# Half 1's keys parked in scratch, and the feed-forward start, splits and late norms put in another order

## The chip, the cores and the metric

The kernel runs on one core of a Trainium2 chip. TensorE (PE) multiplies matrices into PSUM, VectorE (DVE), ScalarE (ACT) and GpSimd (POOL) work on tiles, and SyncE (SP) issues the DMAs, in program order. The metric is the device time of one launch in microseconds (us). Three runs of the kernel before took 3108.89, 3109.24 and 3113.45 us.

## The reference

A transformer block whose norms are scaled and shifted by rows from a condition `c`: attention of 32 query heads over 16 key/value heads (the last 512 cached positions of 2048), then a gated feed-forward network. x is 2048 x 576, Dh is 128, F is 4608, all float32.

```python
q = (x @ wq) ... ; k, v = last W = 512 positions of the caches, each for two query heads
o = softmax(q k^T * Dh ** -0.5) v ; attention = o @ wo
h = sigmoid(x @ w_gate) * (x @ w_up) ; ffn = h @ w_down
...
mod = silu(c) @ w_mod                    # sa, ca, ga, sb, cb, gb
x = x + ga * attention(layernorm(x) * (1 + ca) + sa)
x = x + gb * ffn(layernorm(x) * (1 + cb) + sb)
```

## The kernel before

The 2048 rows are four blocks of 512. Every float32 matmul is made of three products of a "hi" part (the value rounded to fp32r) and a "lo" part (the rest): hi times hi, hi times lo, lo times hi. So each operand is split: mostly ACT copies it to hi and DVE or POOL subtracts to get lo.

**Attention** runs in two halves, half 0 for blocks 0 and 1, half 1 for blocks 2 and 3. A half goes through 32 heads, and the work of one head and one block (a "block step") is four steps n; `at_n(n, fn)` (L426 to L501) lists what is issued besides at step n: loads of weights, splits, norms. A group gg is one key/value head of one half. `load_k` and `load_v` fetch it from the caches, `make_k` (`prep_k`) transposes the keys on PE (L330) and splits them into the tile `kt`, `make_v` splits the values into `vs`. Both halves do this for all 16 heads. At the same time background jobs read the feed-forward weights, form their sums, split them and store them in scratch (`wsc` for gate and up, `dsc` for down).

**Feed-forward** runs in two pairs of blocks, pair 0 and pair 1, with a Strassen-like scheme: seven combinations of the norm's quadrants ("combos" 0 to 6, in the order B11, B21, T1, T2, B22, T3, T4) and seven combinations of the weights. Scratch `scr[pair][c]` holds combo c in rows. `stage` (L741) loads it in two halves into tiles `ts` (three buffers), and `load_combo` (L749) transposes it on PE (L756, twelve transposes), copies to hi on ACT (L757) and subtracts to lo on DVE (L759), giving the tile `hc`. A unit u (36 for each pair) makes seven products (`product`, seven matmuls of 512 columns at L882) from weight tiles `sw` and the `hc` of one combo, into PSUM tiles a, b and c; after two of the seven matmuls it also issues a down-projection (`down`, three matmuls of 288 columns, operands `sd` and `hl`, added on DVE at L854). `keep` copies a PSUM tile to SBUF on ACT (L889); L1003 and L1016 are the sigmoids.

Two units give the four value quadrants A11, A12, A21, A22. `sum_val` forms S1 to S4 from them on POOL (L818), and `split_val` splits values and sums into `hl`: hi on ACT (L812), lo on POOL (L813).

**Pair 1's norm.** `late_stats` (L893) makes the mean and the reciprocal root of blocks 2 and 3 at the end of unit 0, in two chains of 128x4 operations on DVE (L166 to L182), and stores the blocks (`park_x`, L566). `late_tile` (L901) normalises one of four tiles ahead of units 4, 9, 14 and 19 and stores its combos into `scr[1]`.

A scheduler may move instructions on an engine, except those that `pin` or `keep_order` hold in written order. Here the ACT instructions of the feed-forward part are free.

Of the kernel before, what the change touches and what calls it, by code (L numbers as in the profile page):

```python
# [16 lines left out]
P = 128  # L17
# [7 lines left out]
def adaln_block_kernel(ctx: ExitStack, tc: tile.TileContext, x, k_cache, v_cache, wq, wo, w_gate, w_up, w_down,  # L25
# [529 lines left out]
    PH = {}  # L555

# [131 lines left out]

    def mod_make2(key, m, j, add):
        if j == 0:  # L690
            rows2[key] = mod_rows(key + "2", wp if key == "gate" else const)
        mod_make(rows2[key], m, j, add)
# [48 lines left out]
    def stage(pair, c):  # L741
        halves = []
        for i in range(2):
            t = fh.tile([P, 2, D3], F32, tag="ts", name="ts", bufs=3)
            nc.sync.dma_start(t, scr[pair][c][:, 2 * i : 2 * i + 2, :])
            halves.append(t)
        STG[pair, c] = halves

    def load_combo(pair, c):  # L749
        halves = STG.pop((pair, c))  # L750
        hc = fh.tile([P, 5, BLK], F32R, tag="hc", name="hc", bufs=7)
        HC[c] = hc
        for s in range(3):
            p = fpsum("w", 4, [P, BLK])
            for i in range(TPB):
                nc.tensor.transpose(p[:, i * P : (i + 1) * P], halves[i // 2][:, i % 2, s * P : (s + 1) * P], ident)  # L756
# [52 lines left out]
    def split_val(g, a):  # L809
        v = VAL[g, a]  # L810
        hl = fp.tile([P, 2, BLK], F32R, tag="hl", name="hl", bufs=7)
        nc.scalar.activation(hl[:, 0, :], v, AF.Copy)  # L812
        nc.gpsimd.tensor_sub(hl[:, 1, :], v, f32(hl[:, 0, :]))  # L813
        HL[g, a] = hl
# [58 lines left out]
    def product(u, a, c, p, first, downs=(2, 5)):  # L873
        w, h = SW.pop((u, a)), HC[c]
        pairs = []
        for s in range(2):
            pairs.append((w[:, 2 * s, :], h[:, 3 + s, :]))
            pairs.append((w[:, 2 * s + 1, :], h[:, s, :]))
            pairs.append((w[:, 2 * s, :], h[:, s, :]))
        pairs.append((w[:, 4, :], h[:, 2, :]))  # L880
        for n, (l, r) in enumerate(pairs):
            nc.tensor.matmul(p, l, r, start=first and n == 0, stop=n == len(pairs) - 1, skip_group_check=not first)  # L882
            if n in downs:
                down_some(1)
        load_w()

    def keep(p, tag, bufs):
        t = val(tag, bufs)
        nc.scalar.activation(t, p, AF.Copy)  # L889
        return t  # L890


    def late_stats():  # L893
        for b in range(HB, NB):
            for t in range(TPB):
                ln_stats(b, t, True)
            ln_rsqrt(b)
            park_x(b)

    def late_tile(t):  # L900
# [5 lines left out]
        for i, h in enumerate((h0, h1)):  # L906
            mv, y = LN[HB + i]
            nc.vector.tensor_scalar(h, h, mv[:, t, 0:1], y[:, t : t + 1], op0=OP.subtract, op1=OP.mult)
            nc.gpsimd.tensor_mul(h, h, rows2["scale"])
            nc.gpsimd.tensor_add(h, h, rows2["shift"])  # L910
# [7 lines left out]
        put(0, h0[:, lo])  # L918
        put(1, h0[:, hi])
        nc.gpsimd.tensor_sub(ts_[:, lo], h1[:, lo], h0[:, lo])  # L920
        nc.gpsimd.tensor_sub(ts_[:, hi], h1[:, hi], ts_[:, lo])
        put(2, ts_[:, lo])
        put(3, ts_[:, hi])
        put(4, h1[:, hi])
        nc.gpsimd.tensor_sub(h1[:, lo], h1[:, hi], h1[:, lo])
        put(5, h1[:, lo])
        nc.gpsimd.tensor_sub(h0[:, lo], h0[:, hi], ts_[:, hi])
        put(6, h0[:, lo])

    stage(0, 0)  # L930
    stage(0, 1)
    for c in range(7):
        load_combo(0, c)
        if c + 2 < 7:
            stage(0, c + 2)
        if c:
            load_w()
    for _ in range(4):
        load_w()
# [3 lines left out]
    back = later = None  # L943
    for u in range(U + 1):
        pair = u // NF
        nxt = (u + 1) // NF if (u + 1) % NF == 0 and u + 1 < U else None
        if u in (4, 9, 14, 19):
            late_tile((u - 4) // 5)
# [6 lines left out]
        def swap(c, to):  # L955
            if to:
# [11 lines left out]
        if u > 0:  # L968
# [10 lines left out]
            elif u % 2:  # L979
# [23 lines left out]
        nc.scalar.activation(g0, g0, AF.Sigmoid)  # L1003
# [12 lines left out]
        nc.scalar.activation(g1, g1, AF.Sigmoid)  # L1016
# [4 lines left out]
        if u == 0:  # L1021
            late_stats()
# [8 lines left out]
        else:  # L1031
# [3 lines left out]
            split_val(g, S1)  # L1035
# [30 lines left out]
```

## Time and profile before

| what | number |
|---|---|
| median of three runs | 3109.24 us |
| the profiled execution | 3113.13 us |
| its span | 3111.3 us |
| opening, attention half 0, half 1 | 0 to 60, to about 830, to 1833 us |
| feed-forward pairs 0 and 1 | 1833 to 2460, to 3111 us |
| waits ended by ACT for tile c at L882, all units | 11.4 us |
| HBM read, written | 357.83 MB, 140.48 MB |

The span is what the engines' instructions cover; the execution's own time is 1.8 us longer. In the profile a row of the timeline gives the start, the length, the engine, the line, the operation with its tiles and the count; what stands in brackets is the engine's idle time before the row and what ended it. Where PE has no such bracket for a long stretch, the time of that stretch is PE's work.

### The profile page before, as it was taken

What the parts mean: (1) busy time and instruction counts of PE and PEld (TensorE: products, weight loads), DVE (VectorE), ACT (ScalarE), POOL (GpSimd) and SP (SyncE); (2) the same over time, 40 slices, a digit from 0 to 9 for tenths busy, and PEclk for the clock granted to TensorE, in tenths of its full rate; (3) what the DMA queues carried; (4) which work ended last, traced back from release to release, by engine and by line L of the source; (5) the groups of instructions that cost most, each with busy time, mean ns of one, the idle gap of its engine ahead of it and who ended that gap; (6) DMA issues with size and microseconds to landing.
All of it is one profiled execution on the core that took longest, in us unless ns stands there. A gap on an engine that the chain in (4) does not pass through costs nothing.

```text
span 3111.3 us, 49123 instructions
## 1 busy us (share of the span) xinstructions
PE 3058.9 (98%) x17012; PEld 2646.9 (85%) x17012; DVE 2161.7 (69%) x4202; ACT 1432.4 (46%) x2862; POOL 1517.0 (49%) x1610
## 2 busy tenths in 40 slices
PE   7999999999999999999999999999999999999998
PEld 6888888888888888888888877888888888888887
DVE  7777777777888777777777776555555665555556
ACT  4656655555555555555555542232332323323332
POOL 3656655555333545565565505653443444434444
PEclk9999999999999999999999999999999999999999
DMA  4566655665312345444444446886666776666663
GB/s 130 160 168 159 168 156 155 161 160 155 106 31 72 96 116 152 126 119 118 114 124 116 114 166 200 279 254 198 197 199 198 220 247 198 199 198 199 201 198 119
DMA packets 564728, 501.58 MB, mean 161 GB/s; under 512 B 181504, under 2 KB 444672, under 8 KB 563456
## 3 DMA queue, kind: packets, MB, share of 16 engines
q1 hardware_dynamic: 564480, 498.44, 55.5%
q8 instruction: 135, 2.21, 0.3%
q14 instruction: 113, 0.93, 0.1%
HBM read 357.83 MB, written 140.48 MB: 160 GB/s over the span
## 4 chain that ended last, share of the span: by engine, by line
PE 90%; issue 3%; DMA 2%; DVE 2%; POOL 2%; ACT 1%; SPq 0%; POOLq 0%; DVEq 0%; ACTq 0%
PE a L882 14%; PE qp L256 13%; PE wo L256 12%; PE w L256 12%; PE ot L256 11%; PE st L256 11%; PE c L882 7%; PE st L387 7%; PE b L882 3%; POOL hl L813 0%; DVE xp L854 0%; PE st L330 0%; DMA sw<-wsc 0%; POOL vs L818 0%; DMA xp<-in_A_x_dram 0%
## 5 line engine op out<-in xcount | busy, mean ns | idle before, releaser
L854 DVE TENSOR_TENSOR xp<-w,xp 128x288 f32<-128x288 f32 x980 | 443.9, 456 | 464.4 <-PE w L256 463.2
L256 PE MATMUL wo<-wb,ov 128*128 128x288 f32 x3072 | 616.3, 308 | 2.2 <-DVE ov L405 1.2
L390 ACT ACTIVATE ptt<-st 128x512 fp32r<-128x512 f32 x512 | 305.8, 597 | 634.0 <-PE st L387 633.6
L256 PEld LDWEIGHTS w<-sd,hl 128*128 128x128 f32 x3036 | 513.8, 189 | 89.5 <-POOL hl L813 4.9
L882 PE MATMUL a<-hc,sw 128*128 128x512 f32 x2016 | 583.6, 394 | 3.1 <-DVE v L1019 2.2
L256 PE MATMUL w<-sd,hl 128*128 128x288 f32 x3036 | 565.4, 296 | 3.3 <-POOL hl L813 2.8
L414 DVE SCALAR_TENSOR_TENSOR xp<-wo,rs,xp 128x288 f32<-128x288 f32 x1024 | 513.6, 512 | 56.8 <-PE wo L256 8.8
L369 DVE TENSOR_REDUCE neg<-st 128x1 f32<-128x512 f32 x512 | 351.9, 687 | 276.5 <-PE st L256 275.4
L256 PEld LDWEIGHTS wo<-wb,ov 128*128 128x128 f32 x3072 | 482.3, 189 | 51.2 <-DVE ov L405 1.9
L256 PE MATMUL qp<-hTm,wa 128*128 128x512 f32 x1536 | 445.1, 398 | 4.2 <-ACT wa L219 1.4
L256 PE MATMUL ot<-ptt,vs 128*128 128x512 f32 x1536 | 443.8, 396 | 0.1
L256 PE MATMUL st<-kt,qt 128*128 128x512 f32 x1536 | 437.5, 393 | 0.2 <-DVE ptt L391 0.2
L882 PEld LDWEIGHTS a<-hc,sw 128*128 128x128 f32 x2016 | 355.9, 188 | 42.5 <-DVE v L1019 3.4
L375 ACT ACTIVATE pp<-st,neg 128x512 f32<-128x512 f32 x512 | 350.5, 685 | 55.6 <-DVE neg L369 54.6
L662 POOL TENSOR_TENSOR xp<-xp 128x896 fp32r<-128x896 f32 (+2 forms) x135 | 260.6, 1931 | 201.7 <-ACT xp L657 189.8
L391 DVE TENSOR_TENSOR ptt<-st,ptt 128x512 fp32r<-128x512 f32 x512 | 348.3, 680 | 5.3 <-ACT ptt L390 5.2
L256 PEld LDWEIGHTS st<-kt,qt 128*128 128x128 f32 x1536 | 287.5, 188 | 63.0 <-DVE ptt L391 1.0
L882 PE MATMUL c<-hc,sw 128*128 128x512 f32 x1008 | 306.1, 397 | 11.4 <-ACT v L889 11.4
L387 PEld LDWEIGHTS st<-ident,pp 128*128 128x128 f32 x2048 | 254.0, 139 | 73.0 <-ACT pp L375 5.9
L387 PE MATMUL st<-ident,pp 128*128 128x128 f32 x2048 | 306.5, 272 | 2.8 <-ACT pp L375 2.8
L256 PEld LDWEIGHTS qp<-hTm,wa 128*128 128x128 f32 x1536 | 262.0, 189 | 30.9 <-DVE qt L353 2.1
L256 PEld LDWEIGHTS ot<-ptt,vs 128*128 128x128 f32 x1536 | 259.6, 188 | 23.2 <-DVE ptt L391 0.3
(135 smaller groups left out, 3585.9 us busy)
## 6 DMA issues: line engine op xcount, KB each, us to landing
sw<-wsc SPq DMA_DIRECT2D x504, 320.0 KB
sd<-dsc SPq DMA_DIRECT2D x249, 288.0 KB
wsc<-xp SPq DMA_DIRECT2D x144, 448.0 KB
dsc<-xp SPq DMA_DIRECT2D x102, 336.0 KB
raw<-in_A_wo_dram SPq DMA_DIRECT2D x64, 288.0 KB
raw<-in_A_wq_dram SPq DMA_DIRECT2D x64, 256.0 KB
wsc<-xp SPq DMA_DIRECT2D x144, 112.0 KB
ts<-scr SPq DMA_DIRECT2D x28, 384.0 KB
```

What stands on the lines that cost most here:

```text
L256: nc.tensor.matmul(p, l, r, start=first and n == 0, stop=last and n == len(pairs) - 1)
L369: nc.vector.tensor_reduce(NEG[b][:, i : i + 1], p, axis=AX.X, op=OP.max, negate=True)
L375: keep_order(nc.scalar.activation(PP[n], ST.pop(n), AF.Exp, bias=NEG[b][:, i : i + 1], accum_out=SUM[b][:, i : i + 1]))
L387: nc.tensor.transpose(p[:, k * P : (k + 1) * P], PP[n][:, k * P : (k + 1) * P], ident)
L390: keep_order(nc.scalar.activation(PT[b][:, 0, :, cols], pv_, AF.Copy))
L391: nc.vector.tensor_sub(PT[b][:, 1, :, cols], pv_, f32(PT[b][:, 0, :, cols]))
L414: nc.vector.scalar_tensor_tensor(xv, p, RS[b][:, i : i + 1], xv, op0=OP.mult, op1=OP.add)
L662: pin(nc.gpsimd.tensor_sub(v[:, :n].bitcast(F32R), v[:, :n], hi[:, :n]))
L854: nc.vector.tensor_add(acc, p, acc)
L882: nc.tensor.matmul(p, l, r, start=first and n == 0, stop=n == len(pairs) - 1, skip_group_check=not first)
```

## The change

Five parts, which touch each other in the order of the code.

1. Half 0 stores each split key and value tile to scratch (`park_k`, `park_v`), and half 1 fetches them (`fetch_k` eleven steps ahead, `fetch_v` eight) in place of loading, transposing and splitting again.
2. Combos 0 to 2 of pair 0 are loaded at steps N-8 to N-6 into the space of `xp[0]` (`stage_early`). At the start of the feed-forward part `park_x` of blocks 2 and 3 stands ahead of the loads, only combos 0 and 1 are transposed up front, and in unit 0 each product is followed by the transposes of the combo two further on. The first seven `sd` loads go out ahead of the `ts` of combos 5 and 6.
3. All ACT instructions of the feed-forward part are pinned.
4. The splits of S1 to S4 are collected in `later` and issued behind v1's keep. In the last group of a pair the down-projections go by value for the first three.
5. `late_stats` and `late_tile` are one generator, `late_work`; `late_some` issues one of its operations behind each product (two in unit 1), and the root chain runs once, eight wide. In pair 1's staging a fourth buffer (`rows_ss`, which held the scale and shift rows) takes every fourth half.

```diff
@@ -448,17 +448,34 @@
+    kscr = dram.tile([HKV, P, 2, W], F32, tag="kscr", name="kscr")
+    vscr = dram.tile([HKV, P, 2, KT, DH], F32, tag="vscr", name="vscr")
+
     def load_k(gg):
-        KR[gg] = load_kv(k_cache, gg % HKV)
+        KR[gg] = load_kv(k_cache, gg)
 
     def make_k(gg):
         KS[gg] = prep_k(KR.pop(gg))
 
+    def park_k(gg):
+        keep_order(nc.sync.dma_start(kscr[gg], f32(KS[gg])))
+
+    def fetch_k(gg):
+        KS[gg] = at.tile([P, 2, W], F32R, tag="kt", name="kt", bufs=2)
+        keep_order(nc.sync.dma_start(f32(KS[gg]), kscr[gg - HKV]))
...
+    def park_v(gg):
+        keep_order(nc.sync.dma_start(vscr[gg], f32(VS[gg])))
+
+    def fetch_v(gg):
+        VS[gg] = at.tile([P, 2, KT, DH], F32R, tag="vs", name="vs", bufs=2)
+        keep_order(nc.sync.dma_start(f32(VS[gg]), vscr[gg - HKV]))
...
     for gg in range(2 * HKV):
         n = TPB * first_g[gg]
+        if gg >= HKV:
+            at_n(n - 11, fetch_k, gg)
+            at_n(n - 8, fetch_v, gg)
+            continue
+        at_n(n + 2, park_k, gg)
+        at_n(n + 3, park_v, gg)
...
+    first_ts = {}
+
+    def stage_early(c):
+        v = xp[0].rearrange("p b t d -> p (b t d)")[:, c * TPB * D3 : (c + 1) * TPB * D3]
+        v = v.rearrange("p (t d) -> p t d", t=TPB)
+        pin(nc.sync.dma_start(v, scr[0][c]))
+        first_ts[c] = [v[:, 0:2], v[:, 2:4]]
+
+    for c_ in range(3):
+        at_n(N - 8 + c_, stage_early, c_)
...
+            if pair and (2 * c + i) % 4 == 3:
+                t = rows_ss.rearrange("p a d -> p (a d)")[:, : 2 * D3].rearrange("p (t d) -> p t d", t=2)
+            else:
+                t = fh.tile([P, 2, D3], F32, tag="ts", name="ts", bufs=3)
...
-            nc.scalar.activation(hc[:, s, :], p, AF.Copy)
+            pin(nc.scalar.activation(hc[:, s, :], p, AF.Copy))
...
+        late_some(2 if u == 1 else 1)
         load_w()
...
     def late_stats():
-        for b in range(HB, NB):
+        for i in range(HB):
             for t in range(TPB):
-                ln_stats(b, t, True)
-            ln_rsqrt(b)
-            park_x(b)
+                st = const.tile([P, 2, 6], F32, tag="st", name="st", bufs=2)
+                for j in range(2):
+                    yield nc.vector.bn_stats(st[:, j, :], xs[HB + i][:, t, j * D2 : (j + 1) * D2])
+                nc.vector.bn_aggr(mv_l[:, i * TPB + t, :], st)
+            LN[HB + i] = mv_l[:, i * TPB : (i + 1) * TPB], y_l[:, i * TPB : (i + 1) * TPB]
+        v = fp.tile([P, 2 * TPB], F32, name="v_l")
+        a = fp.tile([P, 2 * TPB], F32, name="a_l")
+        yield nc.vector.tensor_scalar(v, mv_l[:, :, 1], EPS, None, op0=OP.add)
+        yi, vi = y_l.bitcast(I32), v.bitcast(I32)
+        yield nc.vector.tensor_scalar(yi, vi, 1, None, op0=OP.logical_shift_right)
+        yield nc.vector.tensor_scalar(yi, yi, -1.0, float(0x5F3759DF), op0=OP.mult, op1=OP.add)
+        for _ in range(3):
+            yield nc.vector.tensor_mul(a, y_l, y_l)
+            yield nc.vector.scalar_tensor_tensor(a, a, -0.5, v, op0=OP.mult, op1=OP.mult)
+            yield nc.vector.scalar_tensor_tensor(y_l, a, 1.5, y_l, op0=OP.add, op1=OP.mult)
...
+    def late_some(k):
+        for _ in range(k):
+            i = next(late, None)
+            if i is not None:
+                pin(i)
...
+    for c_ in first_ts:
+        STG[0, c_] = first_ts[c_]
+    for b in range(HB, NB):
+        park_x(b)
+    stage(0, 3)
+    for c_ in range(2):
+        load_combo(0, c_)
+    for _ in range(5):
+        load_w()
+    stage(0, 4)
+    for _ in range(5):
         load_w()
     for _ in range(7):
         load_sd()
...
+    def split_later():
+        for ga in later:
+            split_val(*ga)
+        later.clear()
...
-        if u in (4, 9, 14, 19):
-            late_tile((u - 4) // 5)
...
+            if u == 0 and c + 2 < 7:
+                load_combo(0, c + 2)
+                if 5 <= c + 4 < 7:
+                    stage(0, c + 4)
...
                 sum_val(g, S3, "-", A11, A21)
-                split_val(g, S3)
+                later.append((g, S3))
             else:
                 VAL[g, A12] = v
                 split_val(g, A12)
-                split_val(g, S2)
                 sum_val(g, S4, "-", A12, S2)
-                if g % NG == NG - 1 or g == GL - 1:
-                    split_val(g, S4)
+                later += [(g, S1), (g, S2), (g, S4)]
+                if g == GL - 1:
+                    split_later()
                     todo += [(g, a, t) for t in range(TPB) for a in ORDER]
+                elif g % NG == NG - 1:
+                    todo += [(g, a, t) for a in ORDER[:3] for t in range(TPB)]
+                    todo += [(g, a, t) for t in range(TPB) for a in ORDER[3:]]
                 else:
-                    later = g
                     todo += [(g, a, t) for a in ORDER for t in range(TPB)]
...
         v1 = keep(pc, "v1", 2)
-        if later is not None:
-            split_val(later, S4)
-            later = None
+        split_later()
...
-        if u == 0:
-            late_stats()
...
             sum_val(g, S1, "+", A21, A22)
-            split_val(g, S1)
             sum_val(g, S2, "-", S1, A11)
```

On PE, where attention ends and feed-forward begins. `wo` is the out-projection, L756 the transposes of combo rows, L882 the products. Before:

```order
L256 MATMUL wo<-wb,ov 128x288 x27
L756 MATMUL w<-ident,ts 128x128 x16
L882 MATMUL a<-hc,sw 128x512
L756 MATMUL w<-ident,ts 128x128 x2
L882 MATMUL a<-hc,sw 128x512 x4
L756 MATMUL w<-ident,ts 128x128 x6
L882 MATMUL a<-hc,sw 128x512 x2
L756 MATMUL w<-ident,ts 128x128 x12
L882 MATMUL b<-hc,sw 128x512 x6
```

The same place in the changed kernel, where these lines are L794 and L920, and `xp_109` holds the early combos:

```order
L256 MATMUL wo<-wb,ov 128x288 x27
L794 MATMUL w<-ident,xp_109 128x128 x36
L794 MATMUL w<-ident,ts 128x128 x4
L920 MATMUL a<-hc,sw 128x512 x7
L920 MATMUL b<-hc,sw 128x512 x7
L794 MATMUL w<-ident,ts 128x128 x4
L920 MATMUL c<-hc,sw 128x512
L794 MATMUL w<-ident,ts 128x128 x4
L920 MATMUL c<-hc,sw 128x512 x6
L794 MATMUL w<-ident,ts 128x128 x6
```

The transposes of three combos now stand in one piece ahead of all products, and two whole products follow without any between them.

On SP at the same place, the queue of DMAs. Before, from the third half tile on:

```order
L745 DMA ts<-scr_260 128x768
L779 DMA sw<-wsc_266 128x640
L745 DMA ts<-scr_260 128x768 x3
L779 DMA sw<-wsc_266 128x640
L745 DMA ts<-scr_260 128x768
L779 DMA sw<-wsc_266 128x640 x2
L745 DMA ts<-scr_260 128x768 x3
L779 DMA sw<-wsc_266 128x640 x4
L802 DMA sd<-dsc_275 128x576 x7
```

In the changed kernel, where L590 is `park_x`:

```order
L590 DMA xscr_266<-xp_110 128x2304
L783 DMA ts<-scr_262 128x768
L590 DMA xscr_267<-xp_110 128x2304
L783 DMA ts<-scr_262 128x768
L817 DMA sw<-wsc_269 128x640 x5
L783 DMA ts<-scr_262 128x768
L817 DMA sw<-wsc_269 128x640 x2
L783 DMA ts<-scr_262 128x768
L817 DMA sw<-wsc_269 128x640 x3
L840 DMA sd<-dsc_278 128x576 x7
L817 DMA sw<-wsc_269 128x640 x2
L783 DMA ts<-scr_262 128x768 x2
```

Both stores of blocks 2 and 3 (1152 KB each) moved ahead of the first weight tile, and the seven `sd` loads moved ahead of the last two half tiles shown, which are combo 5's.

On ACT, behind the border of the pairs, the last splits of pair 0. Before:

```order
L889 ACTIVATE g_28290<-a 128x512
L812 ACTIVATE hl<-g_28089 128x512
L812 ACTIVATE hl<-vs 128x512 x2
L1003 ACTIVATE g_28290<-g_28290 128x512
L889 ACTIVATE v_28381<-c 128x512
L889 ACTIVATE g_28405<-a 128x512
```

In the changed kernel, with L850 for L812, L928 for L889 and L1084 for L1003:

```order
L928 ACTIVATE g_28116<-a 128x512
L850 ACTIVATE hl<-g_27912 128x512
L1084 ACTIVATE g_28116<-g_28116 128x512
L928 ACTIVATE v_28204<-c 128x512
L850 ACTIVATE hl<-vs 128x512 x3
L928 ACTIVATE g_28234<-a 128x512
```

The splits of the sums (`vs`) moved from ahead of the sigmoid and v1's keep to behind both.

More of the change, by code (lines that the diff above doesn't have):

```diff
@@ L555, in adaln_block_kernel @@
     PH = {}
+    rows_ss = const.tile([P, 2, D], F32, name="rows_ss")
     def early_norm(t):
@@ L687, in adaln_block_kernel @@
         at_n(n + 8, bg_store, k, 1)
+    first_ts = {}
[6 more added lines that the diff above has]
+        at_n(N - 8 + c_, stage_early, c_)
     def mod_make2(key, m, j, add):
         if j == 0:
-            rows2[key] = mod_rows(key + "2", wp if key == "gate" else const)
+            rows2[key] = mod_rows("gate2", wp) if key == "gate" else rows_ss[:, 0 if key == "scale" else 1, :]
         mod_make(rows2[key], m, j, add)
@@ L811, in split_val @@
         hl = fp.tile([P, 2, BLK], F32R, tag="hl", name="hl", bufs=7)
-        nc.scalar.activation(hl[:, 0, :], v, AF.Copy)
+        pin(nc.scalar.activation(hl[:, 0, :], v, AF.Copy))
         nc.gpsimd.tensor_sub(hl[:, 1, :], v, f32(hl[:, 0, :]))
@@ L888, in keep @@
         t = val(tag, bufs)
-        nc.scalar.activation(t, p, AF.Copy)
+        pin(nc.scalar.activation(t, p, AF.Copy))
         return t
+    mv_l = const.tile([P, 2 * TPB, 2], F32, name="mv_l")
+    y_l = const.tile([P, 2 * TPB], F32, name="y_l")
     def late_stats():
-        for b in range(HB, NB):
+        for i in range(HB):
             for t in range(TPB):
-                ln_stats(b, t, True)
-            ln_rsqrt(b)
-            park_x(b)
+                st = const.tile([P, 2, 6], F32, tag="st", name="st", bufs=2)
[18 more added lines that the diff above has]
+                pin(i)
     def late_tile(t):
@@ L908, in late_tile @@
             nc.vector.tensor_scalar(h, h, mv[:, t, 0:1], y[:, t : t + 1], op0=OP.subtract, op1=OP.mult)
-            nc.gpsimd.tensor_mul(h, h, rows2["scale"])
-            nc.gpsimd.tensor_add(h, h, rows2["shift"])
+            yield nc.gpsimd.tensor_mul(h, h, rows2["scale"])
+            yield nc.gpsimd.tensor_add(h, h, rows2["shift"])
         def put(c, v):
@@ L918, in late_tile, with late_work @@
         put(0, h0[:, lo])
+        yield nc.gpsimd.tensor_sub(ts_[:, lo], h1[:, lo], h0[:, lo])
         put(1, h0[:, hi])
-        nc.gpsimd.tensor_sub(ts_[:, lo], h1[:, lo], h0[:, lo])
-        nc.gpsimd.tensor_sub(ts_[:, hi], h1[:, hi], ts_[:, lo])
         put(2, ts_[:, lo])
+        yield nc.gpsimd.tensor_sub(ts_[:, hi], h1[:, hi], ts_[:, lo])
         put(3, ts_[:, hi])
         put(4, h1[:, hi])
-        nc.gpsimd.tensor_sub(h1[:, lo], h1[:, hi], h1[:, lo])
+        yield nc.gpsimd.tensor_sub(h1[:, lo], h1[:, hi], h1[:, lo])
         put(5, h1[:, lo])
-        nc.gpsimd.tensor_sub(h0[:, lo], h0[:, hi], ts_[:, hi])
+        yield nc.gpsimd.tensor_sub(h0[:, lo], h0[:, hi], ts_[:, hi])
         put(6, h0[:, lo])
[L930 to L938, printed above, removed]
+        for _ in range(3):
+            yield None
+    def late_work():
+        yield from late_stats()
+        for t in range(TPB):
+            yield from late_tile(t)
+    late = late_work()
+    for c_ in first_ts:
[9 more added lines that the diff above has]
+    for _ in range(5):
         load_w()
@@ L941, in adaln_block_kernel @@
         load_sd()
-    back = later = None
+    back, later = None, []
+    def split_later():
+        for ga in later:
+            split_val(*ga)
+        later.clear()
     for u in range(U + 1):
@@ L1002, in adaln_block_kernel @@
         nc.vector.tensor_add(g0, pb, g0)
-        nc.scalar.activation(g0, g0, AF.Sigmoid)
+        pin(nc.scalar.activation(g0, g0, AF.Sigmoid))
         product(u, S1, T1, pc, True, downs)
@@ L1015, in adaln_block_kernel @@
         nc.vector.tensor_add(g1, pc, g1)
-        nc.scalar.activation(g1, g1, AF.Sigmoid)
+        pin(nc.scalar.activation(g1, g1, AF.Sigmoid))
         product(u, S3, T3, pa, False, downs)
```

3 lines of the change are left out of this document (1 added, 2 removed).

## The prediction

> **What bounds the kernel now.** I read the page's shares first, then the chain of waits, then the stretches, and last PE's timeline where a stretch isn't full. The two lines below are the busy time of each engine and the engines' shares of the chain that ended last.
>
> ```profile
> PE 3058.9 (98%) x17012; PEld 2646.9 (85%) x17012; DVE 2161.7 (69%) x4202; ACT 1432.4 (46%) x2862; POOL 1517.0 (49%) x1610
> PE 90%; issue 3%; DMA 2%; DVE 2%; POOL 2%; ACT 1%; SPq 0%; POOLq 0%; DVEq 0%; ACTq 0%
> ```
>
> PE is busy in all but 52.4 of 3111.3 us, so time falls only with matmul work that goes, or with one of these idle stretches and the low clock behind it. The next rows are stretches: from:to, length, then busy time (and count) of PE, PE's loads, DVE, ACT and POOL, granted clock, DMA share, GB/s.
>
> ```profile
> 140.00:300.00 160.00, 158.82 (x906) 137.19 (x906) 120.25 (x224) 97.24 (x203) 91.83 (x107) 1.00 0.64 167
> 940.00:1760.00 820.00, 819.99 (x4685) 710.11 (x4684) 628.54 (x1191) 465.35 (x986) 453.07 (x590) 1.00 0.44 116
> 1856.00:1860.00 4.00, 3.43 (x18) 2.69 (x17) 1.98 (x3) 2.53 (x5) 0.00 (x0) 0.67 0.94 313
> 1860.00:1864.00 4.00, 4.00 (x19) 3.41 (x18) 3.72 (x7) 1.59 (x4) 0.00 (x0) 0.90 1.02 392
> 1888.00:1892.00 4.00, 0.72 (x2) 0.62 (x3) 2.41 (x4) 1.60 (x3) 1.46 (x2) 0.51 0.26 101
> 2080.00:2440.00 360.00, 360.00 (x1941) 314.95 (x1941) 199.20 (x404) 109.16 (x182) 149.55 (x119) 1.00 0.67 204
> ```
>
> Attention half 1 (940 to 1760) and the plain feed-forward units (2080 to 2440) have no gap at all. What there is to win lies in half 1's own matmul count and at the borders: around 1832 to 1896, the late norms, the border between the two pairs, the end.
>
> **Keys parked.** In half 1 the change removes, per key/value group, four transposes on PE (L330), and a kt and a vs split. A group lasts four steps. PE's rows give start, length, line, operation, count:
>
> ```profile
> 1633.98 0.63 PE L256 MATMUL qp<-hTm,wa 128*128 128x512 f32 x2
> 1637.51 0.60 PE L330 MATMUL st<-ident,raw 128*128 128x128 f32 x4
> 1648.12 0.63 PE L256 MATMUL qp<-hTm,wa 128*128 128x512 f32 x2
> 1661.85 0.62 PE L256 MATMUL qp<-hTm,wa 128*128 128x512 f32 x2
> ```
>
> The four steps with L330 take 1648.12 - 1633.98 = 14.14 us, the next four without it 13.73. The difference of 0.41 us times 16 groups is **6.6 us**, all on the path because PE has no gap there. The splits on ACT, DVE and POOL lie beside PE and count nothing. What it adds is traffic: 32 tiles of 512 KB written in half 0 (16.8 MB in some 770 us, 22 GB/s on a stage whose busiest stretch moves 167 at a DMA share of 0.64) and 16.8 MB read in half 1 in place of 8.4. Fetches go out 8 to 11 steps of 3.46 us ahead, so 28 us cover a tile that takes under 2 at 313 GB/s. Cost 0 while that cover holds; a late tile would stall PE for its lateness. Range 5 to 7.
>
> **Attention to feed-forward.** These are the rows of PE (the wait before a row stands in brackets, with what ended it), of SP's issues, and of DVE, ACT and POOL at the long wait.
>
> ```profile
> 1832.92 1.69 PE L756 MATMUL w<-ident,ts 128*128 128x128 f32 x14
> 1848.84 0.88 PE L756 MATMUL w<-ident,ts 128*128 128x128 f32 x6 [1.64 <-DMA ts<-scr]
> 1855.70 0.87 PE L756 MATMUL w<-ident,ts 128*128 128x128 f32 x6 [1.23 <-DMA ts<-scr]
> 1860.45 4.75 PE L882 MATMUL a<-hc,sw 128*128 128x512 f32 x19
> 1871.27 1.76 PE L882 MATMUL a<-hc,sw 128*128 128x512 f32 x7
> 1891.28 2.93 PE L882 MATMUL c<-hc,sw 128*128 128x512 f32 x6 [6.99 <-ACT v L889]
> 1895.74 0.56 PE L256 MATMUL w<-sd,hl 128*128 128x288 f32 x3
> 1833.77 3.04 SPq L745 DMA_DIRECT2D ts<-scr  x3
> 1850.34 2.62 SPq L745 DMA_DIRECT2D ts<-scr  x3
> 1855.79 4.54 SPq L802 DMA_DIRECT2D sd<-dsc  x7
> 1872.04 0.17 DVE L180 TENSOR_TENSOR ln_a<-ln_y 128x4 f32<-128x4 f32 x1
> 1882.38 1.21 DVE L181 SCALAR_TENSOR_TENSOR ln_a<-ln_a,ln_v 128x4 f32<-128x4 f32 x1
> 1889.40 0.68 DVE L1002 TENSOR_TENSOR g<-b,g 128x512 f32<-128x512 f32 x1
> 1890.11 0.63 ACT L1003 ACTIVATE g<-g 128x512 f32<-128x512 f32 x1 [3.65 <-DVE g L1002]
> 1882.28 1.29 POOL L813 TENSOR_TENSOR hl<-vs,hl 128x512 fp32r<-128x512 f32 x1
> ```
>
> From 1832.92 to 1895.74 pass 62.8 us. The work in it is 84 transposes at 0.10 (14 in 1.69, less the last one's tail), 136 wide matmuls at 0.23 (seven in 1.76, of which 0.16 lies under the next group) and 24 narrow ones at 0.14: 8.4 + 31 + 3.4 = 42.8. So **20.0 us** are lost: 10.7 before 1860.45 in nine waits for `ts` (the largest quoted) and a clock of 0.67; 9.3 behind it, 6.99 of them the one wait at 1891.28 and most of the rest matmuls at half pace (six in 2.93, where 1.4 would do).
>
> The long wait comes from late_stats. Its 128x4 operations take 0.17 us alone and about 1.2 beside a POOL operation of 1.29, and they stand ahead of L1002 on DVE; L1002 releases the sigmoid, and behind that on ACT stands the keep for which PE waits. In the changed kernel these operations come one or two per product, half as many (eight wide), with written order on ACT: this wait goes, and I leave 1 us of it. One sentence on a rule: the Trainium skill, "SBUF — State Buffer", section "Who interferes with whom", says that a DVE operation with two SBUF inputs and a GpSimd operation that reads SBUF exclude each other for the whole instruction; 0.17 against 1.2 agrees, and by the rule the spread ones would each cost at most the rest of one POOL operation, which adds no term.
>
> The first part doesn't simply go, since SP's queue decides it. Three combos now lie in SBUF early, so 40 transposes run at once. But park_x(3), 1152 KB, needs the last out-projection sum, stands ahead of all `sw` loads, and issues at about 1833.7, where SP's `ts` loads stand in the row of 1833.77. The first product needs 1152 + 384 + 320 KB, 1.9 MB, at 313 to 392 GB/s 5 to 6 us: it starts at about 1840, with 4 us of transposes under it, and **3 us** are lost. Then the `ts` of combo 5 stands behind seven `sd` loads that before went out after it: 1152 + 5 x 384 + 12 x 320 + 7 x 288 KB = 9.1 MB after 1833.7, which lands between 1857 and 1863. PE's work ahead of those transposes is 60 transposes and 49 matmuls, 6.0 + 11.2, and with the 3 us it is done by 1853. Wait 4 to 10, I take **6**, and **2** of slow clock behind it, as behind the wait of 6.99. Combo 6 one more, 0.5 in small waits. Loss 12.5 + 1 = 13.5 against 20.0: gain **6.5**, with ends of 2 (wait 10) and 13 (no wait, 3 + 1 and small ones).
>
> A rule that speaks against the change there: the Trainium skill, "TensorE: Matmul & The Clock Gate", section "The HAM clock gate (the "warmup" mystery)", has PE's clock halved after an idle window of about 3.4 us and full again after as long at work. The 0.51 in the stretch of 1888 to 1892 agrees, the 0.67 of 1856 to 1860 without a wait over 1.64 us doesn't quite. By it a new wait of 6 us would add about 1.7, which is what I charge from the row anyway.
>
> **Late norms and the border of the pairs.**
>
> ```profile
> 1946.71 0.93 PE L882 MATMUL a<-hc,sw 128*128 128x512 f32 x3 [0.81 <-DMA sw<-wsc]
> 2014.18 0.95 PE L882 MATMUL c<-hc,sw 128*128 128x512 f32 x3 [0.58 <-ACT v L889]
> 2464.96 0.87 PE L756 MATMUL w<-ident,ts 128*128 128x128 f32 x6 [0.97 <-DMA ts<-scr]
> 2520.52 1.65 PE L882 MATMUL c<-hc,sw 128*128 128x512 f32 x3 [3.26 <-ACT v L889]
> 2526.39 0.56 PE L256 MATMUL w<-sd,hl 128*128 128x288 f32 x3
> 2518.84 0.63 ACT L812 ACTIVATE hl<-vs 128x512 fp32r<-128x512 f32 x1 [3.81 <-POOL vs L818]
> 2517.54 1.26 POOL L818 TENSOR_TENSOR vs<-g,vs 128x512 f32<-128x512 f32 x1
> 3058.50 0.57 PE L256 MATMUL w<-sd,hl 128*128 128x288 f32 x2 [1.57 <-POOL hl L813]
> ```
>
> Units with a late tile lose 2.6 us in three waits (first and last quoted). Spread over more units they should vanish: **2.0**, from -1 (new, smaller ones) to 2.6. Staging pair 1 waits for `ts` three times, 2.33 us together (largest quoted); a fourth buffer lets those loads start one combo-half earlier, worth **2.0** (1 to 2.3). At 2520.52 PE waits 3.26 for v1's keep and then takes 5.87 us to 2526.39 for ten wide and six narrow matmuls worth 10 x 0.23 + 6 x 0.14 = 3.1: 6.0 lost. The cause stands in the ACT row: the split of S4 waits 3.81 for POOL's sum ahead of the sigmoid and that keep. Now the split stands behind the keep; the sum at 2517.54 is still late, so the keep of g1 may wait a little. Gain **4** (0 to 6). At the end PE waits 1.57 for a lo part on POOL; S1's split is later by a product there, so **-0.5** (-1.5 to 0.5).
>
> **Opening.** The program's order puts the first `qt` on DVE ahead of the last rsqrt operation and the normalising of block 1.
>
> ```profile
> 34.58 0.58 DVE L187 TENSOR_SCALAR h<-xp,mv,ln_y 128x576 f32<-128x576 f32 x1
> 36.27 0.69 DVE L353 SCALAR_TENSOR_TENSOR qt<-qp,qt 128x512 fp32r<-128x512 f32 x1 [1.10 <-ACT qt L352]
> ```
>
> The last rsqrt operation and the one of 34.58 ran ahead of this wait; now they stand behind `qt`, which waits for ACT until 36.27, so the first normalised rows come up to 36.27 + 0.69 - 34.58 = 2.4 us later, some of it under PE's other work: **-1** (-2 to +1).
>
> **Sum.** 6.6 + 6.5 + 2.0 + 2.0 + 4 - 0.5 - 1 = 19.6. Against the profiled run of 3113.13 (its span 3111.3 and 1.8 around it) this is 3093.5. That run lies 3.9 above the median 3109.24, so the forecast is **3089.5**.
>
> **Rivals.** (A) My forecast, with all terms inside their ranges: chance 0.55.
> (B) The border stays bound by DMA and the pair border by POOL: nothing at 1832, nothing at 2520, only the keys, late tiles, `ts` and the small losses, 6.6 + 4 - 1.5 = 9. About 3100. For it speaks that 9.1 MB must land in any order at 313 to 392 GB/s; against it that combos 0 to 2 are read before. Chance 0.2.
> (C) The border flows: combo 5 is in time (13), both border waits go (6): 19.6 + 6.5 + 2 and the opening costs nothing, 3080. Chance 0.15.
> (D) Slower. ACT's written order makes it wait for POOL in every unit pair: three splits of sums now stand between two keeps.
>
> ```profile
> 2331.12 1.29 POOL L818 TENSOR_TENSOR vs<-g,vs 128x512 f32<-128x512 f32 x1
> 2333.92 0.60 ACT L889 ACTIVATE v<-c 128x512 f32<-128x512 f32 x1 [0.32 <-PE c L882]
> 2336.39 0.60 ACT L889 ACTIVATE g<-a 128x512 f32<-128x512 f32 x1 [1.87 <-PE a L882]
> ```
>
> POOL's S4 sum is ready at 2332.41, ACT gets to its split at about 2335.6, and the g1 keep behind it is due at 2336.39, needed a product (2.4 us) later. So this decides once POOL's sum is over 5 us later than here. If it were a POOL operation beyond that, 1.29 us times 36 unit pairs is 46 us, less the gains of 19.6: 3136. Chance 0.05.
> (E) The change gives little: keys' traffic slows half 0's loads by what the transposes save, the border as in B, 6.6 less again: about 3106. Chance 0.05.
>
> **How the numbers follow.** A measurement here tells about 0.2%, 6.2 us: faster means below 3103. A, B, C are faster, E is the same, D slower; of B I give 0.03 to the same. Faster 0.87, same 0.08, slower 0.05. The range leaves out D, E and the outer halves of C: from 3077, where all good ends meet but one, to 3101 at B.
>
> **What would show it.** No L330 after 830 us, and groups of 13.73 us: the keys. PE's first product at 1840, a wait of 4 to 10 us for `ts` before the transposes of combo 5, no wait above 2 us for a keep in unit 0 and at the pair border: the borders. A wait on ACT for a POOL sum in the plain units, with PE idle in 2080 to 2440, would show D. I am wrong if half 0 gets gaps that it lacks in 140 to 300, or if the `sw` loads that park_x(3) holds back come after 1842.

## The result and the profile after

The changed kernel takes 3087.71 us (median of four, 3086.07 to 3090.4) against 3109.06 (median of four by then); the ratio is 0.993 with a 95% interval of 0.9912 to 0.9947. The forecast of 3089.5 was 1.8 us off. The profiled execution took 3086.48 us, its span 3084.7, which is 26.6 less than the span of before: that execution of the kernel before lay 4 us above its median, this one 1.2 below.

The page's busy times and its chain, after:

```profile
PE 3044.7 (99%) x16948; PEld 2637.7 (86%) x16948; DVE 2147.1 (70%) x4174; ACT 1411.1 (46%) x2830; POOL 1502.9 (49%) x1594
PE 94%; DVE 2%; DMA 1%; ACT 1%; issue 1%; POOL 1%; SPq 0%; POOLq 0%; ACTq 0%; DVEq 0%
```

PE idles 40.0 us in place of 52.4, and it is busy 14.2 us less. Only 64 transposes went (16948 against 17012), some 7 us, so busy time fell by another 7. Part of that is matmuls that no longer run at a low clock behind a wait, which the prediction counts; the rest, 4 to 5 us, is a change of PE's pace, for which it has no term (below).

The border, in the timeline of PE and of SP's issues after:

```profile
1819.80 1.91 PE L794 MATMUL w<-ident,xp 128*128 128x128 f32 x16
...
1827.58 1.90 PE L920 MATMUL a<-hc,sw 128*128 128x512 f32 x7 [0.33 <-DMA sw<-wsc]
...
1841.54 0.63 PE L920 MATMUL b<-hc,sw 128*128 128x512 f32 x2
1847.37 3.58 PE L794 MATMUL w<-ident,ts 128*128 128x128 f32 x16 [5.21 <-DMA ts<-scr]
1851.11 0.44 PE L794 MATMUL w<-ident,ts 128*128 128x128 f32 x2 [0.16 <-DVE hc L797]
...
1820.54 0.32 SPq L590 DMA_DIRECT2D xscr<-xp  x1
...
1834.32 3.88 SPq L840 DMA_DIRECT2D sd<-dsc  x7
...
1841.08 1.08 SPq L783 DMA_DIRECT2D ts<-scr  x2
```

The first product comes 7.8 us after the first transposes (7 was forecast), and before the transposes of combo 5 PE waits 5.21 us (6 was forecast), and that `ts` was issued behind seven `sd`. The stretches show the DMA traffic in the wait and the clock behind it:

```profile
1842.00:1848.00 6.00, 0.79 (x4) 0.66 (x4) 0.00 (x0) 0.00 (x0) 0.00 (x0) 0.92 1.04 412
1848.00:1852.00 4.00, 3.84 (x20) 3.03 (x19) 2.17 (x4) 2.15 (x4) 0.00 (x0) 0.70 0.63 201
```

In the wait the DMA engines move 412 GB/s with a share above 1; behind it the granted clock is 0.70, and 16 transposes take 3.58 us where 1.91 do in the row of 1819.80. The Trainium skill, "TensorE: Matmul & The Clock Gate", section "The HAM clock gate (the "warmup" mystery)", has the clock halved after an idle window of some 3.4 us; a wait of 5.21 us with 0.70 behind it agrees.

The following table sets the stages beside one another. Each border is the start of one instruction: the ninth reduction at L369 (opening), the first combo transpose (end of attention), and the product of v1 and g1 on DVE that ends a unit. "Again" are second profiles of the same two kernels.

| stage | before | before again | after | after again |
|---|---|---|---|---|
| opening, to the ninth L369 | 67.34 | 67.86 | 69.77 | 70.61 |
| rest of attention | 1765.58 | 1764.55 | 1750.03 | 1749.99 |
| border, to the end of unit 3 | 82.56 | 82.27 | 75.61 | 78.29 |
| units 4 to 23 (late norms) | 342.14 | 341.03 | 337.99 | 337.72 |
| units 24 to 32 | 152.04 | 151.20 | 152.04 | 152.04 |
| units 33 to 41 (pair border) | 169.97 | 171.33 | 163.70 | 163.75 |
| units 42 to 69 | 470.40 | 473.01 | 473.01 | 473.01 |
| rest | 61.30 | 60.83 | 62.55 | 61.89 |

### The profile page after: what moved, and what is told of

Its sections match the earlier page's. It is cut to its first block, busy times and chain, and to the rows that moved or that the text cites. A ratio compares the mean times of both kernels' runs of the same rounds, so it can differ in the third digit from the quotient of the medians.

```text
span 3084.7 us, 49017 instructions
## 1 busy us (share of the span) xinstructions
PE 3044.7 (99%) x16948; PEld 2637.7 (86%) x16948; DVE 2147.1 (70%) x4174; ACT 1411.1 (46%) x2830; POOL 1502.9 (49%) x1594
## 4 chain that ended last, share of the span: by engine, by line
PE 94%; DVE 2%; DMA 1%; ACT 1%; issue 1%; POOL 1%; SPq 0%; POOLq 0%; ACTq 0%; DVEq 0%
PE a L920 14%; PE wo L256 13%; PE qp L256 13%; PE w L256 12%; PE ot L256 11%; PE st L256 11%; PE c L920 7%; PE st L387 7%; PE b L920 4%; DVE xp L892 0%; PE w L794 0%; ACT wm L136 0%; DMA raw<-in_A_v_cache_dram 0%; DMA wm<-in_w_mod_dram 0%; POOL wm L139 0%
## 5 line engine op out<-in xcount | busy, mean ns | idle before, releaser
L920 PE MATMUL a<-hc,sw 128*128 128x512 f32 x2016 | 583.6, 395 | 2.1 <-DVE v L1098 1.6
L369 DVE TENSOR_REDUCE neg<-st 128x1 f32<-128x512 f32 x512 | 352.5, 688 | 279.3 <-PE st L256 278.3
L920 PEld LDWEIGHTS a<-hc,sw 128*128 128x128 f32 x2016 | 354.8, 188 | 44.6 <-DVE v L1098 3.3
L920 PE MATMUL c<-hc,sw 128*128 128x512 f32 x1008 | 305.0, 395 | 0.1
```

Of the source, the lines that this page charges most:

```text
L369: nc.vector.tensor_reduce(NEG[b][:, i : i + 1], p, axis=AX.X, op=OP.max, negate=True)
```

## The experiments

In each, the ratio is to runs of the kernel before on the same chip at the same time; the changed kernel, run once more so, had 0.9923 (0.991 to 0.9937).

### What the parked keys are worth, and the pace of PE

Part 1 alone, put into the kernel before (the edit is the first three pieces of the diff; the last is shown):

```diff
+        if gg >= HKV:
+            at_n(n - 11, fetch_k, gg)
+            at_n(n - 8, fetch_v, gg)
+            continue
+        at_n(n + 2, park_k, gg)
+        at_n(n + 3, park_v, gg)
```

> The kernel before with part 1 alone (keys and values of half 1 parked and fetched). In the first pair of profiles a key/value group (16 steps) took 55.31 us in both halves before, and 55.08 in half 0 and 54.62 in half 1 after, so attention lost 7 us more than 16 x 0.41. Theory A (only the transposes count, the rest is a drift of one profiled execution): half 1's groups come to 54.90 and the kernel is 6.6 less 2.4 for the reordered opening, 4 us faster than before. Theory B (parking changes the pace of all attention matmuls): groups of 55.08 and 54.62 again, 10 to 12 us faster than before. The feed-forward part stays as before, with its 6.99 and 3.26 us waits.

Measured 3104.14 us, ratio 0.998 (0.9971 to 0.9989), so 3 to 9 us faster than before. A group of half 1 took 54.88 us against 55.31; half 0 kept its 55.70. (For half 0 this text gives the mean of ten groups, some of which take longer, up to 57.7 us; a plain group takes 55.31 us there too, or 55.07 in the changed kernel, as the expectations have it.) That is theory A: 0.43 us for each of 16 groups, 6.9 in all, and the opening grew by 1.8 to 2.4.

The changed kernel without part 1 (the same pieces taken out):

> The changed kernel without part 1. The order of DVE's first operations is then that of before, so the opening's 2.4 us come back too. Theory A: slower than the changed kernel by 6.6 - 2.4 = 4 us, about 17 us faster than before. Theory B: slower than the changed kernel by 9 to 11 us, and groups of 55.31 us in both halves.

Measured 3093.25 us, ratio 0.9941 (0.9929 to 0.9954): 5.3 us slower than the changed kernel, nearer to A's 4 than to B's 9 to 11. But its half 0 ran at 55.49 us a group and half 1 at 55.07, not at 55.70 and 55.31. So the keys don't set that pace, and both theories missed it.

The changed kernel and the kernel before, once more without any edit:

> The changed kernel once more, unchanged, for a second profile. If the pace of PE belongs to the program (theory B), the groups are 55.08 and 54.62 us and two units of pair 1 take 33.79 us again. If it is of the execution (theory A), these numbers change by 0.3 to 0.6% while waits stay where they are. About 3087.7 us.

> The kernel before once more, for a second profile. Theory B: groups of 55.31 us, two units of pair 0 in 33.79 and of pair 1 in 33.60 as in the first profile. Theory A: other values. About 3109 us, which also tells what the timing can tell apart.

They took 3087.92 and 3109.57 us (the latter's ratio to other runs of itself 0.9985 to 1.0002, which is what the timing can tell). The rows show full stretches of 360 us, that is busy time and count of PE first. The kernel before again:

```profile
300.00:660.00 360.00, 359.66 (x2054) 311.33 (x2053) 271.00 (x502) 216.42 (x448) 207.15 (x238) 1.00 0.60 157
...
2080.00:2440.00 360.00, 360.00 (x1951) 315.27 (x1951) 200.92 (x407) 109.50 (x183) 149.67 (x118) 1.00 0.68 205
2600.00:2960.00 360.00, 360.00 (x1941) 314.88 (x1940) 200.01 (x405) 110.45 (x184) 152.08 (x121) 1.00 0.66 197
```

The changed kernel (first profile), attention and pair 1:

```profile
300.00:660.00 360.00, 359.63 (x2063) 313.02 (x2062) 272.43 (x505) 217.39 (x450) 206.87 (x238) 1.00 0.65 176
...
2600.00:2960.00 360.00, 360.00 (x1940) 313.99 (x1939) 200.59 (x406) 106.91 (x180) 148.77 (x117) 1.00 0.66 198
```

PE is full and at a granted clock of 1.00 in all of them, yet the same instructions come 0.4% denser in the changed kernel's half 0 (2063 in 360 us against 2054). In attention the pace is of the program: 55.70 a group in every profile of the kernel before and of its variants, 55.49 in every one of the changed kernel and its variants. In the feed-forward part it isn't: the kernel before had pair 0 at 16.893 us a unit and pair 1 at 16.800 in one execution, and the other way round in the next (the 1951 and 1941 above), while the changed kernel had 16.893 in both pairs both times.

In attention the difference lies in the matmuls of 512 columns. Over 940 to 1760 us, from the start of one to the start of the next of its kind, those of `qp` took 231.6 ns in the kernel before and 229.6 in the changed kernel without part 1, those of `st` 229.5 and 226.9, those of `ot` 233.1 and 231.7, while the 288-column ones of `wo` got no shorter (147.0 and 147.6).

Whether the place of one tile in SBUF sets the pace was tried on the kernel before, by putting the scale and shift rows where the changed kernel has them:

```diff
+    rows_ss = const.tile([P, 2, D], F32, name="rows_ss")
...
-            rows2[key] = mod_rows(key + "2", wp if key == "gate" else const)
+            rows2[key] = mod_rows("gate2", wp) if key == "gate" else rows_ss[:, 0 if key == "scale" else 1, :]
```

> The kernel before with the second scale and shift rows in one tile rows_ss, made where the changed kernel makes it; no instruction is added or taken away. All four profiles of the changed kernel's family have groups of 55.49 in half 0, those of the kernel before and of part 1 alone 55.70, and removing part 1 didn't bring 55.70 back. Theory C (place of tiles in SBUF sets the pace of attention's matmuls): groups of 55.49 and 55.07 here, some 7 us faster than before. Rival D: the pace is not of this tile: groups of 55.70 and 55.31, about 3109.

Measured 3110.47 us, ratio 1.0002 (0.9993 to 1.0011), groups of 55.71 and 55.31: rival D. The same the other way, the changed kernel without `rows_ss` and with three `ts` buffers:

> The changed kernel without rows_ss: the rows as before and three ts buffers for pair 1. Theory C: attention's groups go back to 55.70 and 54.83, 7 us slower; rival D: they stay at 55.49 and 54.61. Either way the fourth buffer's worth shows at the pair border: waits for ts of 2.3 us back there, as the prediction put it.

Measured 3089.84 us, ratio 0.9931 (0.9919 to 0.9944); groups of 55.49 and 54.61, so D again. At the pair border its PE timeline has the `ts` wait back:

```profile
2434.84 0.88 PE L790 MATMUL w<-ident,ts 128*128 128x128 f32 x6 [1.80 <-DMA ts<-scr]
...
2442.99 0.88 PE L790 MATMUL w<-ident,ts 128*128 128x128 f32 x6 [0.36 <-DMA ts<-scr]
```

Those two are 2.2 us, and units 33 to 41 take 166.07 in place of 163.70: the fourth buffer is worth 2.4. What sets the pace stays open: the other tiles that only the changed kernel has (`mv_l` and `y_l` among them) were not tried.

### What removed the waits for ACT

The changed kernel with the five `pin(...)` around the feed-forward activations taken away (one is shown):

```diff
-        pin(nc.scalar.activation(hl[:, 0, :], v, AF.Copy))
+        nc.scalar.activation(hl[:, 0, :], v, AF.Copy)
```

> The changed kernel with no feed-forward activation pinned. If written order is what keeps the keeps on time at the border, waits for ACT of 3 to 7 us at L920 come back (3 to 9 us slower than the changed kernel). Rival: the moved splits and spread norms do it alone, and the pins only hold what the scheduler would do: within 2 us. A faster time would mean that written order costs something in the plain units.

Measured 3089.19 us, ratio 0.9931 (0.9918 to 0.9943): within 3 us of the changed kernel, less than expected, since the border went 3 to 5 us faster (72.85 us) while the pair border lost 3.3 and units 4 to 23 lost 1.4. The cause that was sought shows in the timeline of the pair border, ACT and then PE:

```profile
2492.82 0.63 ACT L850 ACTIVATE hl<-vs 128x512 fp32r<-128x512 f32 x1 [2.02 <-POOL vs L856]
2493.35 0.61 ACT L1084 ACTIVATE g<-g 128x512 f32<-128x512 f32 x1
2493.87 0.58 ACT L928 ACTIVATE v<-c 128x512 f32<-128x512 f32 x1
...
2494.50 1.65 PE L920 MATMUL c<-hc,sw 128*128 128x512 f32 x3 [3.02 <-ACT v L928]
```

The split of S4 again waits for POOL ahead of the sigmoid and of v1's keep, though the program writes it behind them. With the pins it stands where it is written, as ACT's timeline of the changed kernel shows at the same place:

```profile
2490.78 0.63 ACT L1084 ACTIVATE g<-g 128x512 f32<-128x512 f32 x1 [0.70 <-DVE g L1083]
2491.32 0.58 ACT L928 ACTIVATE v<-c 128x512 f32<-128x512 f32 x1
2491.80 1.14 ACT L850 ACTIVATE hl<-vs 128x512 fp32r<-128x512 f32 x2
2493.18 0.63 ACT L850 ACTIVATE hl<-vs 128x512 fp32r<-128x512 f32 x1 [0.24 <-POOL vs L856]
2493.72 0.58 ACT L928 ACTIVATE g<-a 128x512 f32<-128x512 f32 x1
```

The border at 1832 shows the other side. Without the pins PE waits there 0.36 us for combo 5 in place of 5.21, although the seven `sd` still stand ahead of that `ts` on SP; and in place of the 6.99 us wait of the kernel before there is one of 1.72:

```profile
1847.24 1.85 PE L794 MATMUL w<-ident,ts 128*128 128x128 f32 x12 [0.36 <-DMA ts<-scr]
...
1871.02 0.97 PE L920 MATMUL c<-hc,sw 128*128 128x512 f32 x3 [1.72 <-ACT v L928]
```

Counted from the first combo transpose, those transposes start 1.5 us earlier than in the changed kernel, and PE has work until 3.4 us later: 61 wide matmuls stand ahead of them in place of 49. So written order on ACT is not free: at the border it costs 3 to 5 us.

The opposite edit, pins on the kernel before and nothing else (one of the five is shown):

```diff
-        nc.scalar.activation(t, p, AF.Copy)
+        pin(nc.scalar.activation(t, p, AF.Copy))
```

> The kernel before with the feed-forward activations pinned and nothing else. With the pins gone from the changed kernel the pair border's 3.02 us wait for ACT came back, and old split places with pins gave only 0.96. If written order alone makes the keeps punctual, the 6.99 and 3.26 us waits and the low clock behind them shrink to under 2 us each and the ACT wait in units 4 to 19 goes: 8 to 14 us faster than before, without any other part. Rival: on this kernel written order makes ACT wait for POOL's sums ahead of the keeps (they stand ahead of them here), in the last groups and at the pair border: not faster than by 2 us, or slower.

Measured 3100.35 us, ratio 0.9966 (0.9953 to 0.9978), 7 to 15 us faster than before. The border took 78.41 us, units 4 to 23 337.31 and the pair border 165.13: within 3 us of the changed kernel in each. There is no fourth `ts` buffer in this kernel. The place of the former 6.99 us wait is nearly full:

```profile
1875.00:1895.00 20.00, 19.22 (x98) 16.19 (x97) 19.11 (x51) 6.52 (x11) 10.10 (x8) 1.00 0.85 286
```

DVE's timeline shows what changed. The pins are on ACT alone, but DVE's order is another one too: L1002, which releases the sigmoid, stands ahead of the second chain of 128x4 operations, whose slow ones still take about 1.2 us. In the kernel before it comes behind that chain, at 1889.40.

```profile
1882.78 0.64 DVE L1002 TENSOR_TENSOR g<-b,g 128x512 f32<-128x512 f32 x1
1883.33 1.21 DVE L175 TENSOR_SCALAR ln_v<-mv 128x4 f32<-128x4 f32 x1
```

ACT's timeline at the pair border has the keep at once and the late split behind it, where its wait of 3.13 us holds up only the keep of g1:

```profile
2507.27 0.64 ACT L1003 ACTIVATE g<-g 128x512 f32<-128x512 f32 x1 [1.05 <-DVE g L1002]
2507.81 0.58 ACT L889 ACTIVATE v<-c 128x512 f32<-128x512 f32 x1
2511.52 0.63 ACT L812 ACTIVATE hl<-vs 128x512 fp32r<-128x512 f32 x1 [3.13 <-POOL vs L818]
2512.06 0.58 ACT L889 ACTIVATE g<-a 128x512 f32<-128x512 f32 x1
```

The changed kernel with the sums split at their old places, pinned:

```diff
-                later.append((g, S3))
+                split_val(g, S3)
...
+                split_val(g, S2)
                 sum_val(g, S4, "-", A12, S2)
...
             sum_val(g, S1, "+", A21, A22)
+            split_val(g, S1)
```

> The changed kernel with the sums split at the old places (S1 and S3 at once, S2 ahead of S4's sum, S4 at once in a pair's last group), activations still pinned. If the old place made the wait of 3.26 us and the 2.8 us of low clock behind it, both are back at the pair border, 4 to 6 us there, less about 1 at the end: 3 to 5 us slower, 3091.5. Rival: the pins or the order of the downs removed the wait: no change at the pair border.

Measured 3095.14 us, ratio 0.9945 (0.9932 to 0.9957), 5 to 7 us slower than the changed kernel. But little of it is where it was expected: the pair border lost 1.2 us, units 4 to 23 2.9, and the border 1 to 4; the opening of that profile was 1 to 2 us longer too. The rows of ACT, POOL and PE in a unit with a late tile:

```profile
1962.61 0.63 ACT L850 ACTIVATE hl<-vs 128x512 fp32r<-128x512 f32 x1 [5.13 <-POOL vs L856]
...
1961.29 1.29 POOL L856 TENSOR_TENSOR vs<-g,v 128x512 f32<-128x512 f32 x1
...
1964.30 0.97 PE L920 MATMUL c<-hc,sw 128*128 128x512 f32 x3 [1.38 <-ACT v L928]
```

POOL makes S3 late, since four operations of a late tile stand ahead of it, ACT waits 5.13 us for it, and behind it in written order stand the sigmoid and v1's keep. This is the mechanism of rival D, in two units (1.38 us on PE here, 2.5 in both). So the moved splits are what makes written order safe beside the late tiles; they are not what removed the wait at the pair border.

The changed kernel with late norms in lumps:

```diff
-        late_some(2 if u == 1 else 1)
...
+        if u in (4, 9, 14, 19):
+            for i in late_tile((u - 4) // 5):
+                pass
...
+        if u == 0:
+            for i in late_stats():
+                pass
```

> The changed kernel with the late norms in lumps again: the statistics (one chain, eight wide) at the end of unit 0, a whole tile ahead of units 4, 9, 14 and 19. If the spreading is what removed the idle times of units 4 to 19 and the wait of 6.99 in unit 1, the stretch from the end of unit 3 to that of unit 23 grows from 337.99 by 2 to 4 us, and unit 1 gets a wait for ACT of 3 to 7: 5 to 9 us slower. Rival: halving the chain and pinning did most of it: 2 to 4 us slower.

Measured 3088.75 us, ratio 0.9927 (0.9913 to 0.994): no difference from the changed kernel that the timing can tell. Units 4 to 23 took 337.87 us (337.99 there), and their stretch is full:

```profile
1905.00:2005.00 100.00, 100.00 (x540) 87.45 (x539) 58.94 (x119) 29.43 (x50) 62.52 (x50) 1.00 0.87 254
```

There was no wait for ACT in units 1 and 2 either (the 6.99 us wait of the kernel before is in unit 2). Spreading gave nothing that pins, moved splits and the single chain didn't give already.

### The wait for combo 5

The changed kernel with the first `sd` loads behind the `ts` of combos 5 and 6:

```diff
-    for _ in range(7):
-        load_sd()
...
                     stage(0, c + 4)
+                if c == 2:
+                    for _ in range(7):
+                        load_sd()
```

> The changed kernel with its first seven sd loads issued behind the ts of combos 5 and 6. If the 5.21 us wait for ts at the border comes of SP's order, as the prediction says, it falls under 1 us and the low clock behind it (about 1.5 us) goes too: 5 to 7 us faster than the changed kernel, about 3081.5. Rival: the border is bound by DMA bytes, the sw loads behind sd are late instead, and the wait only moves to a product of unit 0: within 2 us of 3087.7.

Measured 3086.89 us, ratio 0.9923 (0.9909 to 0.9937). That is 1 us faster than the changed kernel, not 5 to 7. The wait for combo 5 fell to 0.82 us and the border to 73.48 us, but units 4 to 23 grew to 342.10, with four waits of 0.5 to 0.9 us for `sw` on PE, two of them these:

```profile
2004.08 1.91 PE L920 MATMUL a<-hc,sw 128*128 128x512 f32 x7 [0.86 <-DMA sw<-wsc]
2006.52 1.89 PE L920 MATMUL b<-hc,sw 128*128 128x512 f32 x7 [0.53 <-DMA sw<-wsc]
```

SP's waits over 1940 to 2020 (total, times, longest) name what stood ahead of those `sw` loads, the store of a late tile that waits for POOL:

```profile
SPq L974 <- POOL h L970: 12.0, 2, 8.2
```

In the changed kernel SP stood at the same store for up to 6.7 us, and no `sw` load came late.

So, with that edit kept, the late tiles were started 28 products later, and each tile's stores put three products behind its sums:

```diff
+        for _ in range(3):
+            yield None
         put(0, h0[:, lo])
...
         yield from late_stats()
+        for _ in range(28):
+            yield None
```

> The kernel with sd behind the ts, with the late tiles started 28 products later and each tile's stores three products behind its sums. There the ts wait at the border was gone, but sw waits of 2.7 us and low clock came up in units 8 to 11, where SP stood 8.2 us at a store that waits for POOL. If that is what gave the gain back, units 4 to 23 return to 337.9 us and the kernel gains 3 to 5 us on the changed one, about 3083.5. Rival: other waits take their place, 3086 to 3088.

Measured 3084.4 us, ratio 0.9912 (0.9898 to 0.9925): the fastest of all, 5.4 us below the variant without `rows_ss` that ran beside it, of which the buffer explains 2.4. Units 4 to 23 are back at 337.61 us and the border takes 71.90. Its intervals overlap with the changed kernel's, so the 3 us between the two rest on the stages and the medians.

## Why the prediction came out right

**Keys.** 6.6 was forecast; e1 shows 0.43 us a group, 6.9, and its attention is 7.4 to 8.4 us shorter behind the opening. Right, though a group has sixteen steps of 3.46 us, not four; L330 stands in it once, so the sum holds. The traffic cost nothing that shows: half 0 kept its 55.70 us with 175 GB/s in place of 157.

**Opening.** 1 us was forecast, -2 to +1; it lost 2.4 in the first pair of profiles, 2.8 in the second, outside the bounds. Without part 1 it is back at 67.65 us (e2), so the new order of DVE's first operations comes of part 1. The rows of DVE and PE after, and last PE's row of before:

```profile
36.56 0.69 DVE L353 SCALAR_TENSOR_TENSOR qt<-qp,qt 128x512 fp32r<-128x512 f32 x1 [1.57 <-ACT qt L352]
...
42.88 0.63 PE L201 MATMUL st<-ident,h 128*128 128x128 f32 x4 [2.12 <-DVE h L189]
...
40.61 0.63 PE L201 MATMUL st<-ident,h 128*128 128x128 f32 x4 [1.26 <-DVE h L189]
```

The mechanism was right and the size off. I counted the 2.4 us by which the first normalised rows slip and took part of it to be covered. But DVE now makes two tiles of rows at a time, the first one's transposes came at 42.88 in place of 40.61, and PE's other work covered little of that.

**Border at 1832.** Gain 6.5 forecast, 7.0 and 4.0 measured in the two pairs of profiles. The waits are those named: first product after 7.8 us, 5.21 us for combo 5 behind the `sd` loads, a clock of 0.70 behind it. e5 confirms that SP's order takes part in the wait for combo 5, but it is not the whole cause: without the pins the wait goes as well (0.36 us in e6), with SP's order as it was. So it takes both, and the prediction named SP's order alone. For the lost 6.99 us wait I named the spread operations and written order together, but both are not needed: e9 loses it by the pins alone, with both chains of 128x4 operations still in one lump, e8 with pins and a lump doesn't get it back, and e6, without pins and with all the rest, has 1.72 us of it left. That the chain ahead of L1002 made the wait fits e9's DVE rows. One reading was wrong: of the nine waits ahead of 1860.45 in the kernel before, six (4.5 us) were for `ts` and three (1.5 us) for `hc` on DVE.

**Late norms.** 2.0 forecast, 3.3 to 4.2 measured. The size was low in part because I counted three waits, 2.6 us, where the first profile of before has four, 3.2 (the fourth is 0.61 at 2065.73); the clock was 1.00 there, so no low clock comes on top, and the rest is not traced. The cause named, spreading, is wrong: lumps cost nothing (e8), and pins on the old lumps gave 337.31 us (e9).

**Pair border.** 2.0 for the buffer, 2.4 measured in e11. For the long wait 4 was forecast. The whole stretch gained 6.3 to 7.6, so about 4 to 5. Here the step failed that reads "now the split stands behind the keep" as an effect of the moved code. The wait is in unit 38 and its S4 that of pair 1's first group, whose split was written behind the keep before as well; the scheduler had drawn it ahead, and does so again when the pins are off (e6). The ACT order shown ahead of the prediction as "the last splits of pair 0" can't be of pair 0 either: behind pair 0's last group, copies to `hc` stand between the keep and the split that are neighbours there.

**End.** -0.5 forecast, -1.1 and -1.25 measured. The cause that I named doesn't account for it. POOL's lo parts hold up down-projections in five places in place of three in the first pair of profiles, but for 2.8 us in all both times, and for 3.3 us in place of 3.6 in the second; PE's wait for v on DVE grew by 0.5, and the rest is open. The longest wait for POOL after:

```profile
3029.61 0.53 PE L256 MATMUL w<-sd,hl 128*128 128x288 f32 x2 [0.97 <-POOL hl L851]
```

**What had no term.** The denser attention, 55.49 us a group against 55.70: e2, where attention's steps are those of before, has a rest of attention 6.6 to 7.6 us shorter (1825.63 to its end less 67.65 of opening). Against it, the first profile of before had pair 1 at 16.800 us a unit, so units 42 to 69 look 2.6 us longer after. In the first pair of profiles attention behind the opening gave 15.55 where 6.6 was forecast, the late norms 2.15 more than forecast and the two borders 0.7; against that the pace of pair 1 took 2.6, the opening 1.4 and the end 0.75 more. That makes the 7 us by which the profiled span fell further than the 19.6 forecast. So some 7 of the 21 us gained come of attention's pace, whose cause is open; about 3 are lost again in the feed-forward part, where the kernel before had one pair of 36 units at 16.800 in both profiles and the changed kernel none. That the forecast of 19.7 stands so near to the 21.35 of the medians is in part luck: terms of several us that were missing or mis-sized offset each other, and the profiled executions lie further apart than the medians.

**Rivals.** B fails on both borders, C on the wait for combo 5. D did not come true in the changed kernel, whose plain units are full, but e7 shows its mechanism two units long. E fails on half 0, which kept its pace under the added writes.

## What to carry to other kernels

Where a scheduler may reorder an engine, look at the order it made before blaming the work: pinning 5 lines of ScalarE was worth 7 to 15 us on the kernel before. Then measure the pins again in the final kernel: in the rearranged code the same five were worth 1 to 3 us, which is within the noise, since they also let PE wait for combo 5. A pinned engine needs its late inputs moved behind its urgent outputs, else it waits for them (5.13 us for one sum). On a DMA queue, moving a load behind another gains only if what stands further back isn't near its limit too: when the first 5 us wait went, four smaller ones came, and the stage behind took 4.1 us more.

## What the runs showed of the hardware

With PE busy without a gap and the granted clock at 1.00, the same sequence of matmuls ran at different paces: 16.893 or 16.800 us a feed-forward unit, and 16.847 throughout pair 1 of the changed kernel without pins (e6); 55.70 or 55.49 us a group in attention's half 0. A pace holds for hundreds of us. In the feed-forward part of the kernel before, the two pairs swapped their paces from one profiled execution to the next; in attention a program kept one. In attention the place of `rows_ss` isn't the cause (e10, e11), nor are the parked keys (e1, e2) or the pins of the feed-forward part (e6, e9). Worth up to 7 us of 3100, this is more than several terms of a careful sum, and it stays open.
